# A list scheduler in the source sets the order of every queue of a fused attention and MLP kernel

## The chip, the cores and the metric

The kernel runs on one core of a Trainium2 chip. The metric is the device time of one execution in microseconds. TensorE (PE), VectorE (DVE), ScalarE (ACT), GpSimd (POOL) and SyncE (SP) each work through a queue of their own in order; a wait at the head of a queue holds everything behind it. All DMAs of this kernel are issued by SyncE.

## The reference, cut to what matters

```python
def mab(q, kv):                      # x: 4 x 12480 x 128, inducing: 32 x 128
    s = scale * (q @ kv.T); s = s - s.max(-1)
    a = np.exp(s); a /= a.sum(-1) + 1e-9
    return a @ kv
h = mab(I, x)                        # per batch: 32 x 128
attn = mab(x, h)                     # per batch: 12480 x 128
out = (np.maximum(attn @ w_in, 0) ** 2) @ w_out     # d_ff = 2048
```

The first attention reduces a whole batch to 32 rows h, so nothing of a batch's second half can start before its h is complete. The second attention gives every token 32 weights that sum to one.

## The kernel before, in words

A batch has 26 chunks of 480 tokens (CH), in 7 groups of four (the last of two). The kernel never forms the 2048 hidden columns: since each token is a mix of the 32 rows of h, the squared sum is a form in products of pairs of the 32 weights. There are five kinds of work.

1. **First attention** of batch b (`first`): scores of seven groups (matmuls on x transposed, `xp`), a maximum, exponentials on ScalarE, 32x32 transposes on VectorE (line 356), and row sums on TensorE against the rows of x (line 368), which arrive in 13 half-tiles through five buffers `xnb`. Its end is `hT` (line 385).
2. **Preparation** of batch b (`prepare`): from h and the weights to `w16` (pair weights, four sets of products, line 540, and of sums, line 548), `lin`, `singles`, `osc` and `bias`; long chains of small VectorE steps between TensorE steps.
3. **Second attention** of each group (`second`): scores against h and their transpose into one of 8 slots (line 405), maximum (408), subtraction on POOL (412), exponential (413), sums (416 to 418), product on POOL (419), transpose (422), split into two halves (428, 431), and a store to DRAM `ad` (432).
4. **Squares** of each group (`squares`): three loads of `ad` back as `dT` (450), a matmul (464), VectorE (470), POOL (474), and four stores into `dT` (476).
5. **Chunks** (`Chunk`): two `up` steps of two matmuls into a pair of PSUM banks each (658; there are two pairs), two `lift` steps on ScalarE that square them (668), `down` with five matmuls (674, 675), an eviction with scale and bias on ScalarE (678) or VectorE (680), and a store (681) from a ring of three.

The order is made in two layers. The source emits the chunks in a loop and sprinkles the steps of kinds 1 to 4 between them: a planner (`spread`, `plan`, `background`) gives each step a date in units of chunks, and `background(k)` emits what has come due. `heavy` says by chunk number whether an eviction goes to ScalarE. The framework's own scheduler then sets each queue's order with its model of time; `issue_after` only keeps background steps behind their anchors on the same engine. Batch 0's first attention, with the narrowing of the weights, lies ahead of all this, and batch 0's preparation and first two groups come right behind its h. All loads of the next batch (`xp`, lines 272; rows, 261 and 265) share SyncE's queue with the chunks' stores.

Of the kernel before, what the change touches and what calls it, by code (L numbers as in the profile page):

```python
# [13 lines left out]
AF = mybir.ActivationFunctionType  # L14
ALU = mybir.AluOpType
AX = mybir.AxisListType

P = 128
# [30 lines left out]
def attend_then_relu2_mlp(ctx: ExitStack, tc: tile.TileContext, xn, xT, indT, w_in, w_out, outT):  # L49
# [218 lines left out]
    def load_xT(b, G, again=False):  # L268
        pool, bufs = (mlp, 2) if again else (flow, NX)
        w = WID[G]  # L270
        xp = pool.tile([P, 4 * CH], F32, tag="xp", name=f"xp_{b}_{G}_{again}", bufs=bufs)[:, 0:4 * w]
        nc.sync.dma_start(xp, xT[:, b, 4 * CH * G:4 * CH * G + 4 * w])
        return xp
# [7 lines left out]
    def first(b):  # L281
# [5 lines left out]

        def load_xn(h):

            return load_half(b, h, xnb[h % XB]) if h < HALVES else None  # L290
# [20 lines left out]
        xns = st.rows if not b else {}  # L311
        for G, w in enumerate(WID):
            if b and G == 3:
                xns = {h: load_xn(h) for h in range(XB)}
            if not b:
                turn(G)
# [36 lines left out]
        for G, nb32 in enumerate(BLK):  # L353
# [9 lines left out]
            for t in range(nb32):  # L363
# [7 lines left out]
                if b and (t % 8 == 7 or t == nb32 - 1):  # L371
                    xns[h + XB] = load_xn(h + XB)
# [15 lines left out]
    def second(b, G, again=False):  # L388
# [4 lines left out]
        xp = st.xp.pop(G)  # L393
# [3 lines left out]
        scores(ps, st.hT, xp, w)  # L397

        if again:
            e = work.tile([P, 15, MI], F32, tag="e2", name=f"e2_{b}_{G}")  # L400
        else:
            k = 480 * ((NG * b + G) % SLOTS)
            e = scored[:, k:k + 480].rearrange("p (t i) -> p t i", i=MI)
        ef = e.rearrange("p t i -> p (t i)")
        nc.vector.transpose(ef[:, 0:wb], ps[:, 0:wb])  # L405
        yield
        mx = work.tile([P, 15], F32, tag="mx2", name=f"mx2_{b}_{G}")
        nc.vector.tensor_reduce(mx[:, 0:t], e[:, 0:t], axis=AX.X, op=ALU.max)  # L408
        held["act"] += 100 + 0.833 * wb
        held["dve"] += 5 * (110 + 1.042 * wb) + 400  # L410
        yield
        nc.gpsimd.tensor_tensor(e[:, 0:t], e[:, 0:t], mx[:, 0:t].unsqueeze(2).broadcast_to([P, t, MI]), op=ALU.subtract)  # L412
        nc.scalar.activation(e[:, 0:t], e[:, 0:t], AF.Exp, scale=scale)  # L413
        yield
        z = work.tile([P, 15], F32, tag="z2", name=f"z2_{b}_{G}")
# [4 lines left out]
        yield  # L420
# [3 lines left out]
        if again:  # L424
            nc.scalar.copy(a16[:, 0, 0:w], a[:, 0:w])
            nc.vector.tensor_tensor(a16[:, 1, 0:w], a[:, 0:w], a16[:, 0, 0:w], op=ALU.subtract)
        else:
            nc.vector.tensor_scalar(
                a16[:, 0, 0:w], a[:, 0:w], lessen, None, op0=ALU.add, op1=ALU.min, accum_out=least_d[:, b, G:G + 1],
            )  # L430
            nc.vector.scalar_tensor_tensor(a16[:, 1, 0:w], a[:, 0:w], lessen, a16[:, 0, 0:w], op0=ALU.add, op1=ALU.subtract)
        nc.sync.dma_start(st.ad[:, :, :, 480 * G:480 * G + w].rearrange("q i h n -> (q i) h n"), a16[:, :, 0:w])
        yield
# [20 lines left out]

    def squares(b, G):

        st = sts[b]
        n = GRP[G]
        rows = slice(0, MI * n)
        dT = st.aT[G] = load_dT(b, G)  # L460
        yield
        ps = ps_o.tile([P, 512], F32, tag="po", name=f"sq_{b}_{G}")
        for j in range(n):
            nc.tensor.matmul(  # L464
                ps[MI * j:MI * j + MI, 0:CH].rearrange("p (q t) -> p q t", q=4), st.singles[0:96],
                dT[0:96, :, j * TP:(j + 1) * TP], start=True, stop=True,
            )
        z = mlp.tile([P, CH], F32, tag="z", name=f"z_{b}_{G}", bufs=2)
        held["dve"] += 110 + 1.042 * CH
        nc.vector.tensor_scalar(z[rows], ps[rows, 0:CH], st.off[rows], cut[rows], op0=ALU.add, op1=ALU.max)  # L470
        yield
        g = mlp.tile([P, 4, TP], F16, tag="zz", name=f"zz_{b}_{G}", bufs=2)
        zv = z.rearrange("p (q t) -> p q t", q=4)
        nc.gpsimd.tensor_tensor(g[rows], zv[rows], zv[rows], op=ALU.mult)  # L474
        for j in range(n):
            nc.sync.dma_start(dT[96:P, :, j * TP:(j + 1) * TP], g[MI * j:MI * j + MI])
        yield

    def prepare(b):

        st = sts[b]
        tt, ts, stt = nc.vector.tensor_tensor, nc.vector.tensor_scalar, nc.vector.scalar_tensor_tensor
        held["dve"] += 16000

        ps = side_psum(f"hw_{b}")
        scores(ps, st.hT, w_in_sb, 512)
        hw = flow.tile([P, NF, MI], F32, tag="hw", name=f"hw_{b}", bufs=1)
        nc.vector.transpose(hw.rearrange("p k i -> p (k i)"), ps)
        hws = flow.tile([P, NF, MI], F32, tag="hws", name=f"hws_{b}", bufs=1)
        ssq = small("ssq")  # L490
        nc.scalar.activation(hws.rearrange("p k i -> p (k i)"), ps, AF.Square, accum_out=ssq)
        yield
        ends = work.tile([P, 2, NF], F32, tag="ends", name=f"ends_{b}")
        hi, lo, sm = ends[:, 0], ends[:, 1], small("sum_c", NF)
        cm2 = small("cm2", 3)
        nc.vector.tensor_reduce(sm, hw, axis=AX.X, op=ALU.add)
        bank = side_psum(f"bank_{b}")
        bp = bank[:, 500:508]
        nc.tensor.matmul(bp[:, 0:1], every, ssq, start=True, stop=True)
        mg, nmg, s, k2 = small("mg"), small("nmg"), small("s"), small("k2")  # L500
        root(k2, bp[:, 0:1], 2.0 ** 62)
        nc.vector.reciprocal(s, k2)
        yield
        hw16 = flow.tile([P, NF, 2, MI], F16, tag="hw16", name=f"hw16_{b}", bufs=1)
        for k in range(2):
            nc.scalar.mul(hw16[:, :, k], hw, s)
        hw16f = hw16.rearrange("p k q i -> p k (q i)")
        nc.vector.tensor_reduce(hi, hw, axis=AX.X, op=ALU.max)
        nc.vector.tensor_reduce(lo, hw, axis=AX.X, op=ALU.min)
        ts(hws, hw, s, None, op0=ALU.mult)  # L510
        yield
        ts(mg, k2, 2.0 ** -20, None, op0=ALU.mult)
        ts(nmg, k2, -2.0 ** -20, None, op0=ALU.mult)
        up, dn, pos, mix, inc = (small(n, NF) for n in ("up_c", "dn_c", "pos", "mix", "inc"))
        mean = (1.0 - RHO) / MI
        ts(dn, lo, 0.0, RHO, op0=ALU.min, op1=ALU.mult)
        stt(dn, sm, mean, dn, op0=ALU.mult, op1=ALU.add)
        stt(dn, dn, nmg, lo, op0=ALU.add, op1=ALU.max)
        ts(pos, dn, 0.0, None, op0=ALU.is_ge)
        sp = small("sp", NF)  # L520
        stt(sp, sm, s, pos, op0=ALU.mult, op1=ALU.mult)
# [12 lines left out]
        def products(c):  # L534
# [6 lines left out]
            if c == NQ - 1:  # L541
                nc.vector.tensor_copy(g[:, :, 112:P], hwS[:, :, 0:16])
# [483 lines left out]
```

## Time and profile before

| | us |
|---|---|
| median of 3 runs (lowest, highest) | 431.45 (429.72, 433.61) |
| profiled execution | 429.16 |
| its span, first to last instruction | 427.4 |
| TensorE, VectorE, ScalarE, POOL busy | 355.8, 314.5, 298.4, 86.8 |

Busy time adds the records of one engine without counting overlap twice. TensorE's matmuls are pipelined, so its busy time covers some time in which nothing more was issued than the next matmul needed. The chain of waits follows back from the last instruction to what released each step. In rows of the trace `PE hp L658 x4` is four matmuls of line 658 that write `hp`; `xp_False` is `xp` of batches 1 to 3.

### The profile page before, as it was taken

How to read it: one execution, taken by the hardware profiler on the slowest of the kernel's cores; microseconds unless marked ns; L12 is line 12 of the kernel's file. 1: busy time of each engine (PE TensorE's matmuls, PEld its weight loads, DVE VectorE, ACT ScalarE, POOL GpSimd, SP SyncE). 2: the span in 40 equal slices, each digit the busy share in tenths (PEclk: the TensorE clock that was granted, in tenths of full speed). 3: DMA queues.
4: the chain of work that ended last, by engine and by line, in shares of the span. 5: the costliest groups of instructions: out<-in, count | busy, mean ns of one | idle time of the engine just before them, and what ended most of it. 6: DMA issues, size and time to landing. Idle time of an engine off the chain costs nothing.

```text
span 427.4 us, 8743 instructions
## 1 busy us (share of the span) xinstructions
PE 355.8 (83%) x3077; PEld 169.3 (40%) x3077; DVE 314.5 (74%) x857; ACT 298.4 (70%) x416; POOL 86.8 (20%) x93
## 2 busy tenths in 40 slices
PE   0994648599949989798799698998998898999993
PEld 0753413253414433244444233354443344544441
DVE  8859899969711499999444899995169999664441
ACT  1564330068948887677756798788798997899983
POOL 1000021522100032522000334320014442211000
PEclk9996985679969999999999999999999999999998
DMA  7972666915689786796799797976863256556542
GB/s 276 416 237 76 224 205 234 269 46 160 187 300 307 253 290 207 245 266 198 216 339 294 263 377 259 232 250 210 292 197 96 83 180 196 178 168 187 156 163 99
DMA packets 63765, 94.34 MB, mean 221 GB/s; under 512 B 22880, under 2 KB 53856, under 8 KB 63712
## 3 DMA queue, kind: packets, MB, share of 16 engines
q1 hardware_dynamic: 63712, 93.69, 68.1%
q8 instruction: 26, 0.43, 0.4%
q14 instruction: 27, 0.22, 0.2%
HBM read 58.52 MB, written 31.95 MB: 212 GB/s over the span
## 4 chain that ended last, share of the span: by engine, by line
PE 42%; DVE 29%; DMA 16%; ACT 5%; issue 3%; SPq 2%; POOL 1%; DVEq 0%; ACTq 0%
PE hp L658 13%; PE po L674 12%; DMA xnb<-xn_dram 6%; DMA outT_dram<-o 4%; PE hacc L368 4%; DVE G L540 4%; PE s L277 4%; ACT g L668 3%; PE po L675 3%; PE wq L548 3%; DMA rows<-xn_dram 3%; DVE scored L405 3%; DVE z L416 2%; DMA dT<-ad 2%; DVE mx L408 2%
## 5 line engine op out<-in xcount | busy, mean ns | idle before, releaser
L668 ACT ACTIVATE g<-hp 128x960 f16<-128x960 f32 x208 | 195.1, 973 | 44.6 <-PE hp L658 37.2
L658 PE MATMUL hp<-dT,pairs 96*128 96x480 f16 x416 | 119.0, 371 | 3.4 <-ACT g L668 3.3
L674 PE MATMUL po<-g,w 128*128 128x480 f16 x416 | 113.8, 367 | 3.4 <-DVE z L470 1.8
L474 POOL TENSOR_TENSOR zz<-z 128x480 f16<-128x480 f32 (+1 forms) x28 | 29.5, 1054 | 161.7 <-DVE z L470 107.6
L674 PEld LDWEIGHTS <-w 128*128 128x128 f16 x416 | 39.1, 98 | 53.8 <-issue 15.3
L678 ACT ACTIVATE o<-po,bias,osc 128x480 f32<-128x480 f32 x66 | 49.6, 757 | 12.5 <-DMA outT_dram<-o 8.1
L658 PEld LDWEIGHTS <-pairs 96*128 96x128 f16 x416 | 35.0, 99 | 58.3 <-issue 34.3
L680 DVE TENSOR_SCALAR o<-po,osc,bias 128x480 f32<-128x480 f32 x38 | 29.5, 775 | 35.0 <-PE po L675 27.8
L412 POOL TENSOR_TENSOR scored<-scored,mx 128x480 f32<-128x480 f32 (+1 forms) x28 | 29.6, 1057 | 115.1 <-DVE k L197 56.3
L368 PE MATMUL hacc<-xnb,en 128*32 128x128 f32 x664 | 27.7, 292 | 13.6 <-DMA xnb<-xn_dram 10.6
L675 PE MATMUL po<-dT,lin 128*128 128x480 f16 x104 | 38.2, 367 | 0.0
L419 POOL TENSOR_TENSOR scored<-scored,z 128x480 f32<-128x480 f32 (+1 forms) x28 | 27.2, 972 | 44.8 <-DVE z L418 30.4
L356 DVE STREAM_TRANSPOSE en<-sT 128x480 f32<-128x480 f32 (+1 forms) x28 | 17.7, 638 | 23.8 <-PE hacc L368 22.0
L540 DVE TENSOR_TENSOR G<-hwp,hw 128x512 f16<-128x512 f16 x64 | 28.3, 501 | 1.1 <-PE wq L548 1.1
L413 ACT ACTIVATE scored<-scored 128x480 f32<-128x480 f32 (+1 forms) x28 | 16.2, 579 | 18.3 <-POOL scored L412 18.3
L368 PEld LDWEIGHTS hacc<-xnb,en 128*32 128x32 f32 x664 | 18.8, 115 | 25.3 <-DMA xnb<-xn_dram 13.1
L470 DVE TENSOR_SCALAR z<-sq,off,cut 128x480 f32<-128x480 f32 (+1 forms) x28 | 21.4, 765 | 8.2 <-PE sq L464 7.9
L304 ACT COPY xp<-xt 128x896 f32<-128x896 f32 (+1 forms) x13 | 12.3, 956 | 17.1 <-PE xt L301 17.1
L345 ACT ACTIVATE sT<-sT,nb 128x480 f32<-128x480 f32 (+1 forms) x28 | 18.3, 667 | 7.1 <-DVE nb L338 7.1
L277 PE MATMUL s<-xp_False,indT_sb 128*32 128x480 f32 (+1 forms) x168 | 20.5, 561 | 3.2 <-DMA xp_False<-xT_dram 2.3
L277 PE MATMUL s<-xp_False,hT 128*32 128x480 f32 (+1 forms) x168 | 19.9, 547 | 3.3 <-DVE sT L321 3.1
L321 DVE TENSOR_SCALAR_CACHE_REDUCE sT<-s 128x480 f32<-128x480 f32 (+1 forms) x28 | 17.0, 608 | 5.8 <-PE s L277 5.7
(206 smaller groups left out, 456.0 us busy)
## 6 DMA issues: line engine op xcount, KB each, us to landing
outT_dram<-o SPq DMA_DIRECT2D x104, 240.0 KB, 2.6
xp_False<-xT_dram SPq DMA_DIRECT2D x18, 960.0 KB, 5.3
xnb<-xn_dram SPq DMA_DIRECT2D x21, 512.0 KB, 7.0
xnb<-xn_dram SPq DMA_DIRECT2D x23, 448.0 KB, 6.1
dT<-ad SPq DMA_DIRECT2D x72, 120.0 KB, 3.6
ad<-a SPq DMA_DIRECT2D x24, 240.0 KB, 3.1
dT<-zz SPq DMA_DIRECT2D x104, 30.0 KB, 2.3
wi<-w_in_dram SPq DMA_DIRECT2D x4, 512.0 KB, 5.8
```

What stands on the lines that cost most here:

```text
L277: nc.tensor.matmul(ps[32 * q:32 * q + 32, 0:w], lhsT, xp[:, w * q:w * q + w], start=True, stop=True,)
L368: st.last = nc.tensor.matmul(hacc[32 * q:32 * q + 32, 0:P], en[:, t], xg[:, t % 8], start=G == 0 and t < 4, stop=G == NG - 1 and t + 4 >= ...
L412: nc.gpsimd.tensor_tensor(e[:, 0:t], e[:, 0:t], mx[:, 0:t].unsqueeze(2).broadcast_to([P, t, MI]), op=ALU.subtract)
L419: nc.gpsimd.tensor_tensor(e[:, 0:t], e[:, 0:t], z[:, 0:t].unsqueeze(2).broadcast_to([P, t, MI]), op=ALU.mult)
L474: nc.gpsimd.tensor_tensor(g[rows], zv[rows], zv[rows], op=ALU.mult)
L540: tt(g[:, :, MI * j:MI * j + n], hwp[:, :, 0:n], hw16f[:, :, s0:s0 + n], op=ALU.mult)
L658: last = nc.tensor.matmul(hp[:, i, 0:CH].rearrange("p (q t) -> p q t", q=4), pairs[0:96, (2 * j + i) * P:(2 * j + i + 1) * P], self.dT[0:9 ...
L668: return nc.scalar.activation(self.g[:, 2 * j:2 * j + 2], self.hp.pop(j)[:, 0:2, 0:CH], AF.Square)
L674: nc.tensor.matmul(po[:, 0:CH], st.w16[:, i], self.g[:, i], start=i == 0, stop=False)
L675: done = [nc.tensor.matmul(po[:, 0:CH].rearrange("p (q t) -> p q t", q=4), st.lin, self.dT, start=False, stop=True)]
L678: done.append(nc.scalar.activation(o, po[:, 0:CH], AF.Identity, bias=st.bias, scale=st.osc))
L680: done.append(nc.vector.tensor_scalar(o, po[:, 0:CH], st.osc, st.bias, op0=ALU.mult, op1=ALU.add))
```

## The change

The planner, `heavy`, `background` and the `issue_after` anchors go. The five kinds of work are rewritten as jobs: generators that yield before each step the engine, an assumed duration, a due time, and what it needs, and then emit the step's instructions. `Order.run` keeps a clock per engine and for the DMA, finds the earliest time at which any job could go on, and of the jobs that could go on on that engine within PATIENCE of it takes the one due first. The whole stretch from batch 0's h on is emitted in that order, and `manual_schedule` makes the program's order the order of the queues. Buffer rings are modelled (`Ring`), a cross-engine handover costs LATE, a transfer lands after LAND or behind what is queued. An eviction takes ScalarE or VectorE, whichever is free first. Preparation steps are cut finer and put in another order within a batch; `mx2` and `z2` have 4 buffers instead of 2. `prepare_w_out` is emitted ahead of the ordered stretch. The arithmetic, tiles and transfers stay.

```diff
-HEAVY = 18
-READ = (0, 2, 1, 1)
-REST = 2.6
-LONG, LAG, WEIGHTS = 5, 3, 10
+NO = 3
+PERIOD = 2.95
+LEAD = 33.0
+SLACK = 6.0
+AHEAD = 17
+QUEUED = 3.0
+PATIENCE = 0.12
+SPARE = 0.3
+LAND = 3.2
+LATE = {"PE": 0.25, "ACT": 0.2, "DVE": 0.15, "POOL": 0.25}
...
+    def when(self, job):
+        engines, took, due, needs, alone = job[1]
+        t = 0.0 if alone else job[2]
+        for n in needs:
+            r = n.ready()
+            if r is None:
+                return None
+            t = max(t, r)
+        if engines == "SP":
+            return max(t, self.free["SP"], self.moved - QUEUED), "SP"
+        if "|" in engines:
+            act, dve = max(t, self.free["ACT"]), max(t, self.free["DVE"])
+            return (act, "ACT") if act + SPARE < dve else (dve, "DVE")
+        return max(t, self.free[engines]), engines
+
+    def run(self):
...
+            first, engine = min(w for w, _ in could)
+            (start, engine), job = min(
+                ((w, j) for w, j in could if w[1] == engine and w[0] <= first + PATIENCE), key=lambda x: (x[1][1][2], x[0][0]),
+            )
+            took = job[1][1]
+            if engine == "SP":
+                self.free["SP"] = start + 0.06
+                self.moved = max(self.moved, start) + took
+                end = max(start + LAND, self.moved + LAND - 0.7)
+            else:
+                self.free[engine] = start + took
+                end = start + took + LATE[engine]
...
+    def nominal(n):
+        return LEAD + PERIOD * n
+
+    def h_due(b):
+        return nominal(NCH * b - AHEAD)
...
+    def x_loads():
...
+                end = yield op("SP", 2.6 * w / CH, h_due(b) - 30 - 2.0 * (NG - G), xp_ring, alone=True)
+                sts[b].xp[G] = load_xT(b, G, flow, NX)
...
+    def row_loads():
...
+                end = yield op("SP", 1.4, h_due(b) - 24 + 1.3 * h, xnb_free[i], alone=True)
+                sts[b].rows[h] = load_half(b, h, xnb[i])
...
+    def row_sums(b, zs):
...
+                end = yield op("PE", 0.075 * (t1 - t0), H - 14 + 2.0 * G, *needs)
...
+    def readings():
...
+                X = nominal(NCH * b + 4 * G) - 14 - SLACK
+                due = X - 9
+                if b < NB - 1:
+                    due = min(due, h_due(b + 1) - 32 - 2.0 * (NG - G))
+                end = yield op("PE", 0.85, due, att, mark("h", b))
...
+    def attention(b, G, e, X, since, gone):
...
+        yield op("DVE", 0.6, X - 7, here)
...
+        end = yield op("SP", 0.7, X)
...
+    def squares():
...
+                X = nominal(NCH * b + 4 * G) - 11 - SLACK
+                end = yield op("SP", 1.1, X, mark("ad", b, G), dT_ring, alone=True)
...
+    def square(b, G, n, X, rows, dT):
...
+        end = yield op("SP", 0.12 * n, X + 7)
+        for j in range(n):
+            nc.sync.dma_start(dT[96:P, :, j * TP:(j + 1) * TP], g[MI * j:MI * j + MI])
...
+    def pair_weights(b, F, cast, hw16, hw16f, hwp, hwS, pos, since):
...
+            end = yield op("DVE", 1.4 if c < NQ - 1 else 1.6, F - 20 + 4.0 * c, G_ring)
...
+    def pair_sums(b, c, F, g, since):
...
+        end = yield op("PE", 0.93, F - 16 + 4.0 * c, *needs)
...
+    def ups():
...
+                end = yield op("PE", 0.41, nominal(n - 1.5 + j / 2), hp_ring, mark("dT", b, c // 4), alone=True)
...
+    def lifts():
...
+                end = yield op("ACT", 0.92, nominal(n - 1 + j / 2), mark("up", n, j), *([] if j else [g_ring]), alone=True)
...
+    def downs():
...
+            needs = [mark("g", n), mark("zz", b, c // 4), mark("wq", b), mark("lin", b), po_ring]
+            end = yield op("PE", 1.02, nominal(n + 0.8), *needs, alone=True)
...
+    def evictions():
...
+            end = yield op("ACT|DVE" if n < len(CHUNKS) - 1 else "ACT", 0.7, nominal(n + 1.1), mark("down", n), o_ring, alone=True)
...
+    def stores():
...
+            end = yield op("SP", 0.65, nominal(n + 1.5), mark("out", n), alone=True)
...
+    prepare_w_out()
+    for job in (ups(), lifts(), downs(), evictions(), stores(), readings(), squares(), x_loads(), row_loads(), first_softmax(), smallest()):
+        order.add(job)
     for b in range(NB):
...
+        order.add(prepare(b))
+    with tc.manual_schedule(engines={E.PE, E.Activation, E.DVE, E.Pool, E.SP}):
+        order.run()
```

In a preparation F is `nominal(NCH * b)` and the steps' dues run from F - 34 to F - 14. The jobs `exponents`, `transposes` and `row_sums` are the tail of the first attention; each runs at its own pace.

## Rows read from the trace of the kernel before

**Rows 1.** The page's first part: busy us, share of the span, instructions.

```profile
PE 355.8 (83%) x3077; PEld 169.3 (40%) x3077; DVE 314.5 (74%) x857; ACT 298.4 (70%) x416; POOL 86.8 (20%) x93
```

**Rows 2.** Windows of 10 us: busy us (instructions) per engine, granted clock, DMA share, GB/s.

```profile
120.00:130.00 10.00, 5.10 (x42) 2.26 (x43) 0.68 (x1) 3.79 (x5) 0.00 (x0) 0.66 0.87 320
...
220.00:230.00 10.00, 9.58 (x99) 4.64 (x99) 3.91 (x9) 6.69 (x8) 0.97 (x1) 1.00 0.94 261
...
380.00:390.00 10.00, 10.00 (x53) 4.51 (x51) 4.76 (x7) 9.58 (x11) 0.99 (x1) 1.00 0.64 182
```

**Rows 3.** Chain of waits, whole span: start us, us, what.

```profile
202.13 2.23 DMA outT_dram<-o
...
228.92 8.02 DMA outT_dram<-o
...
293.56 6.23 DMA xnb<-xn_dram
...
391.10 0.81 PE po L674 x4
...
404.05 2.24 DMA outT_dram<-o
```

**Rows 4.** Chain of waits, from 52 to 126 us.

```profile
52.49 0.20 DVE hT L385
...
63.38 2.73 DVE G L540 x8
66.11 0.59 DVE scored L405
...
73.81 3.63 DMA ad<-a
...
78.32 7.46 DMA dT<-ad
...
86.51 1.71 PE hp L658 x4
...
90.73 0.94 PE s L277 x8
...
94.72 0.90 PE wq L548 x16
...
98.49 0.20 PE po L675
...
115.93 2.48 PE hacc L368 x73
118.40 6.45 DMA xnb<-xn_dram
```

**Rows 5.** Instructions of lines 476, 681, 450: issue ns min/median/max, first and last start.

```profile
L476 SPq DMA_DIRECT2D dT<-zz x104: 585/600/1710, 88.4 to 409.6; - x104
...
L681 SPq DMA_DIRECT2D outT_dram<-o x104: 332/376/1475, 101.1 to 421.7; - x104
...
L450 SPq DMA_DIRECT2D dT<-ad x84: 303/427/1487, 77.5 to 397.8; - x84
```

**Rows 6.** The page's DMA issues: count, KB each, median us to landing.

```profile
outT_dram<-o SPq DMA_DIRECT2D x104, 240.0 KB, 2.6
...
xnb<-xn_dram SPq DMA_DIRECT2D x21, 512.0 KB, 7.0
...
dT<-ad SPq DMA_DIRECT2D x72, 120.0 KB, 3.6
```

**Rows 7.** Timeline of SyncE's queue ahead of 228 us: start us, us, what.

```profile
227.12 1.38 SPq L261 DMA_DIRECT2D xnb<-xn_dram  x3
```

**Rows 8.** Groups by line: busy us, mean ns; idle before, releasers.

```profile
L668 ACT ACTIVATE g<-hp 128x960 f16<-128x960 f32 x208 | 195.1, 973 | 44.6 <-PE hp L658 37.2 <-PE po L674 5.9 <-ACT g L668 0.3
...
L678 ACT ACTIVATE o<-po,bias,osc 128x480 f32<-128x480 f32 x66 | 49.6, 757 | 12.5 <-DMA outT_dram<-o 8.1 <-PE po L675 3.4 <-ACT g L668 0.6
...
L680 DVE TENSOR_SCALAR o<-po,osc,bias 128x480 f32<-128x480 f32 x38 | 29.5, 775 | 35.0 <-PE po L675 27.8 <-DMA outT_dram<-o 5.4 <-ACT sT L345 1.6
```

More of the change, by code (lines that the diff above doesn't have):

```diff
@@ new lines, with __init__, add, step @@
+class Order:
+    def __init__(self):
+        self.free = {"PE": 0.0, "ACT": 0.0, "DVE": 0.0, "POOL": 0.0, "SP": 0.0}
+        self.moved = 0.0
+        self.jobs = []
+    def add(self, gen):
+        job = [gen, None, 0.0]
+        self.step(job, None)
+    def step(self, job, end):
+        try:
+            job[1] = job[0].send(end)
+        except StopIteration:
+            return
+        if end is not None:
+            job[2] = end
+        self.jobs.append(job)
+    def when(self, job):
[13 more added lines that the diff above has]
+    def run(self):
+        while self.jobs:
+            could = []
+            for job in self.jobs:
+                w = self.when(job)
+                if w:
+                    could.append((w, job))
+            assert could, "every job waits"
+            first, engine = min(w for w, _ in could)
[10 more added lines that the diff above has]
+                end = start + took + LATE[engine]
+            self.jobs = [j for j in self.jobs if j is not job]
+            self.chosen = engine
+            self.step(job, end)
@@ L48, in attend_then_relu2_mlp, with op @@
+def op(engines, took, due, *needs, alone=False):
+    return engines, took, due, needs, alone
 @with_exitstack
@@ L309, in turn @@
                     nc.scalar.copy(to[:, :, 224:240], ps[:, 7].rearrange("p (q r) -> p q r", q=4)[:, :, 0:16])
-        xns = st.rows if not b else {}
+        xns = st.rows
         for G, w in enumerate(WID):
[L313 to L316, printed above, removed]
+            turn(G)
             ps = att_psum(f"s1_{b}_{G}")
@@ L453, in load_dT @@
         return dT
[L455 to L477, printed above, removed]
@@ new lines, in readings @@
+    def readings():
+        for b in range(NB):
+            st = sts[b]
+            for G in range(NG):
+                w, t = WID[G], BLK[G]
+                wb = 32 * t
+                X = nominal(NCH * b + 4 * G) - 14 - SLACK
[3 more added lines that the diff above has]
+                end = yield op("PE", 0.85, due, att, mark("h", b))
+                done = att.take()
+                ps = att_psum(f"s2_{b}_{G}")
+                scores(ps, st.hT, st.xp.pop(G), w)
+                mark("read", b, G).t = end
+                end = yield op("DVE", 0.62, due + 1, slots)
+                gone = slots.take()
+                k = 480 * ((NG * b + G) % SLOTS)
+                e = scored[:, k:k + 480].rearrange("p (t i) -> p t i", i=MI)
+                if wb > w:
+                    nc.vector.memset(ps[:, w:wb], 0.0)
+                nc.vector.transpose(e.rearrange("p t i -> p (t i)")[:, 0:wb], ps[:, 0:wb])
+                done.t = end
+                order.add(attention(b, G, e, X, end, gone))
@@ new lines, in squares @@
+    def squares():
+        for b in range(NB):
+            st = sts[b]
+            for G, n in enumerate(GRP):
+                X = nominal(NCH * b + 4 * G) - 11 - SLACK
+                rows = slice(0, MI * n)
+                end = yield op("SP", 1.1, X, mark("ad", b, G), dT_ring, alone=True)
+                dT_ring.held.append(mark("over", b, G))
+                dT = st.aT[G] = load_dT(b, G)
+                mark("dT", b, G).t = end
+                order.add(square(b, G, n, X, rows, dT))
@@ new lines, in pair_sums @@
+    def pair_sums(b, c, F, g, since):
+        st = sts[b]
+        here = Mark()
+        here.t = since
+        needs = [here, mark("tsg", b), side if c == 0 else mark("wq", b, c - 1)]
+        end = yield op("PE", 0.93, F - 16 + 4.0 * c, *needs)
+        if c == 0:
+            side.held.append(mark("wq free", b))
+            st.wq = side_psum(f"wq_{b}")
+        for k in range(NF):
+            nc.tensor.matmul(st.wq[:, c * P:c * P + P], g[:, k], w_hi[:, k], start=k == 0, stop=k == NF - 1)
+        mark("G used", b, c).t = end
+        mark("wq", b, c).t = end
+        end = yield op("ACT", 0.32, F - 14 + 4.0 * c, *([mark("over", b - 2, NG - 1)] if b > 1 else []))
+        nc.scalar.mul(st.w16[:, c], st.wq[:, c * P:c * P + P], st.tsg[:, c:c + 1])
+        if c == NQ - 1:
+            mark("wq", b).t = end
```

763 lines of the change are left out of this document (450 added, 313 removed).

## The prediction

> **What bounds the kernel now.** I began with the page's busy times: TensorE 355.8 us, VectorE 314.5, ScalarE 298.4 of a 427.4 us span [rows 1]. No engine fills the span, so I read stretches of 10 us next. In 380:390 TensorE is busy throughout and issues 53 matmuls, while ScalarE works 9.58 of 10 us: this is the rate the kernel reaches when nothing disturbs it. In 120:130 TensorE has 5.10 us and VectorE 0.68 [rows 2]. The busy time hides part of the loss, because matmul records overlap; I count TensorE's work by its spacing in the chain of waits instead. Four matmuls of 480 columns take 0.81 us [rows 3], so a chunk (four up, five down) takes 9 x 0.2025 = 1.82 us and 104 chunks 190 us. The 21 + 28 score groups at 0.94 us, seven of them half size, are 43 us; 39 half-tiles of row sums, some 16 matmuls each, at the burst's 2.48 us for 73 are 21 us; four preparations, with 4 x 0.90 us of pair sums each [rows 4] and about 5.6 us of smaller matmuls by my estimate, are 37 us; squares and small products, also estimated, about 14. Together 305 us after batch 0's h.
>
> h is ready at 52.7 us [rows 4], so 374.7 us remain in the span and about 70 us of TensorE time holds no work. I place it in three parts. **Lead**: from h to the end of chunk 0's first complete output at 98.7 [rows 4] are 46 us with some 24 us of work, so 22 lost. **Middle**: from 98.7 to the issue of the last store at 421.7 [rows 5] are 323 us with 281 of work, so 42 lost. **End**: 5.7 us for that store. The chain names the middle: row sums wait for loaded rows three times, 6.45 us first and 6.23 last, 16.7 together; evictions wait for earlier stores to land five times, 2.23 first, 8.02 the longest, 2.24 last, 17.9 together [rows 3, 4]. These are queueing costs, and order is what this change rewrites. By contrast the matmuls, activations and transfers are the same in number and shape; the arithmetic after h must still fit 305 us of TensorE.
>
> **The change, part by part.**
>
> *Before h nothing moves* except that the preparation of w_out comes first in the program. Its two long activations already run before the square of hw, and h's own chain is not behind them. Taken at 0; if its products came later, each late microsecond would shift everything.
>
> *Lead.* In the old order VectorE does, ahead of the first attention store at 73.81 [rows 4], work that the first chunk's input does not need: five further reading transposes (5 x 0.59 from the chain [rows 4]), the rest of group 1's attention (about 3.2), and the first two sets of pair products (2.73 [rows 4]): 8.9 us. By due times, group 0's attention falls due 6 to 12 us after h, those transposes at 16.5 and later, products at 13 and 17. They go behind. The gain for that store is bounded by 0 (POOL and ScalarE steps of group 0 become exposed, and VectorE idles for them) and 8.9; I take 6, nearer the upper end since independent preparation steps fill the gaps. Then the dT load took 7.46 us there [rows 4] against a median of 3.6 [rows 6]: it shared the DMA with five x loads. The new order starts row loads at once and holds queued transfers to 3 us by its own count; gain between 0 and 3.9, taken at 2. First up: 86.5 - 8 = 78.5. The first output also needs the pair weights; on VectorE about 11 us of later groups' work (transposes, maxima, first scores of batch 1) leaves the way, so it moves by the same 8. Of these, 3 us are score matmuls merely moved into the middle. Net **5 us**.
>
> *Row loads.* The five buffers were filled long before, used in one burst of 73 matmuls in 2.48 us, and the sixth half-tile was only issued when the burst had freed a buffer; hence 6.45 us of standstill [rows 4]. The new order knows a landing time (about 3.9 us for a half-tile), and puts chunk matmuls between. The measured median is 7.0 [rows 6], so some 3 us per round stay uncovered; two rounds in three batches would give back all 16.7. But 7.0 includes the burst's own queue: a half-tile at 1.4 us behind four others accounts for it. I take 6 of 16.7 as left: **gain 10.7**, bounds 0 and 16.7.
>
> *Stores.* A store that lands in 2.6 us [rows 6] cannot stall a ring of three outputs; the 8.02 us one was issued right behind three row loads [rows 3, 7]. Loads dealt out one at a time remove most bursts, while stores still share the queue: 6 of 17.9 left, **gain 11.9**, bounds 0 and 17.9.
>
> *Evictions* choose ScalarE or VectorE by which is free 0.3 us earlier, instead of a fixed stretch per batch. The total does not change: 66 at 757 ns and 38 at 775 ns [rows 8], 79 us. With 195.1 us of lifts ScalarE stays under TensorE's 305. Taken at 0, hidden under TensorE; without that cover up to the 3.4 us by which ScalarE's evictions waited for output matmuls [rows 8].
>
> *SyncE.* No DMA is added, but every one has a new place. The scheduler books 0.06 us of SyncE for an operation; four issues of the squares take 4 x 600 ns, three dT issues 3 x 427, a store 376 [rows 5]. With 104, 84 and 104 of these that is 137 us, with the hundred other transfers, at 0.4 to 0.6 by my estimate, some 182 us of issue in 375, so SyncE is half busy and a wrong place costs up to 2.4 us behind one set of squares. Taken inside the 6 + 6 us left above; its larger price is the first rival.
>
> The Trainium skill, Perfetto Trace Analysis, section "What 'DMA-bound' means", counts a DMA sequencer full of issues as a bound of its own. No row here shows SyncE full, so by that rule the sum is unchanged unless the stretch with loads closes up.
>
> *Sum.* 5 + 10.7 + 11.9 = 27.6 us. The profiled execution took 429.16 us with 427.4 in the span; the median of the three runs is 431.45, 2.3 higher. 431.45 - 27.6 = **404 us**. Check: 305 us of TensorE would then lie in 347 us instead of 375, a share of 88% where 81% stood; 380:390 shows that it can hold more than that.
>
> **Rivals.**
>
> *1. SyncE is late (chance 0.16).* At 404 us the issues fill 182 of 347 us on average, but in stretches with loads nearer two thirds. If one set of squares in each of the 21 groups with loads around it puts 1 us on TensorE through a late load or store, 21 us of the 22.6 in the middle go, and only the lead remains: 431.45 - 6.6 = 425 us. For it: 0.60 us for each of four against 0.06 for all [rows 5]. Against: work is due 20 us ahead of use, a slack that swallows 2.4. A bound by issue, as that section of the Trainium skill has it, would show in the same way.
>
> *2. Loads crowd out stores (chance 0.10), slower.* x and row loads become eligible as soon as their buffers are free. Seven x buffers and five row buffers are 9.2 MB; 220:230 moved 261 GB/s with the DMA engines 0.94 busy [rows 2]. The scheduler assumes some 370 GB/s, and nothing on the chip tells it that transfers run late. It decides where a store takes over three chunk times less an eviction, 3 x 3.0 - 0.8 = 8.2 us; the store at 228.92 took 8.02 [rows 3]. If every third store of the three batches with loads (26 of 78) exceeds that by 1.5 us, 39 us are added; less the 27.6 won, 443 us. Against: the old order had such bursts too, and only five stores of it show in the chain.
>
> *3. Little is changed (chance 0.04).* The old planner also had dates, and its queues were already laid out in advance; if the new order is nearly the same one, 431 us.
>
> **How the numbers follow.** The forecast, that at least half of the middle's 34.6 us and some lead go, has 0.70. Its own range is 388 (both waits gone, 34.6, and the lead's upper bounds, 8.9 + 3.9 less 3 moved: 44) to 424 (all lead bounds at 0 and a fifth of the waits). The range of 8 in 10 drops rival 2 and the lowest corner and takes in rivals 1 and 3 up to 430. One per cent, 4.3 us, is what a measurement here can tell from no change. Faster than 427.1: the forecast and 0.07 of rival 1, 0.77. Same: 0.07 of rival 1, 0.03 of 3, 0.02 of 2, 0.12. Slower: the rest, 0.11.
>
> **What would show it.** Right: first up matmul near 78 us after the start and the first complete output near 90; no 6 us wait of row sums on loads, stores in the chain under 10 us in all; no stretch between 100 and 360 with TensorE near 5 us; lifts at 7 to 8 per 10 us there instead of 4 to 7. The lead is wrong if VectorE idles between group 0's steps and the first store stays near 73. Rival 1 shows as engines waiting for transfers whose issue was queued behind squares; rival 2 as stores landing after 8 us or more, evictions waiting on them. The prediction fails altogether if ScalarE, with 195.1 us of lifts, becomes the engine that others wait for: two pairs of PSUM banks hold lifts and up matmuls in step, and an in-order queue that places another activation too early stops both.

## The result: 427.35 us instead of 431.65, and the profile after

| | before | after |
|---|---|---|
| median (lowest, highest), four executions each on one chip | 431.65 (429.72, 433.61) | 427.35 (426.38, 427.44) |
| ratio [95% interval] | | 0.9895 [0.9848, 0.9942] |
| profiled execution, its span | 429.16, 427.4 | 426.38, 424.6 |

The forecast was 404 us, a gain of 27.6 us; the gain was 4.3. The result lies in the stated range, which reached up to 430 us to take in two rivals. Ratios, here and below, leave out executions over 1.5% above the fastest of their kernel. The page's first part, after, against [rows 1]:

```profile
PE 357.0 (84%) x3077; PEld 169.2 (40%) x3077; DVE 329.9 (78%) x879; ACT 285.4 (67%) x394; POOL 83.3 (20%) x93
```

The groups of the lifts and evictions, after (busy us, mean ns | idle before, releasers), against [rows 8]:

```profile
L1059 ACT ACTIVATE g<-hp 128x960 f16<-128x960 f32 x208 | 193.7, 969 | 63.7 <-PE hp L1045 62.5
...
L1093 DVE TENSOR_SCALAR o<-po,osc,bias 128x480 f32<-128x480 f32 x60 | 46.1, 768 | 44.8 <-PE po L1075 34.2 <-DMA outT_dram<-o 3.9 <-PE s L369 3.1
L1091 ACT ACTIVATE o<-po,bias,osc 128x480 f32<-128x480 f32 x44 | 33.1, 755 | 11.2 <-PE po L1075 4.1 <-DMA dT<-ad 2.3 <-DVE a L779 2.2
```

Evictions stand 44 to 60 where they stood 66 to 38, and ScalarE waits 62.5 us for up matmuls instead of 37.2. No engine fills the span; TensorE's share, 84%, is the highest. The chain of waits, after (start us, us, what): the lead, then all its waits for a DMA behind the lead, against [rows 3, 4].

```profile
53.53 1.06 PE hw L369 x8
...
77.81 0.89 PE hp L1045 x2
...
88.96 0.20 PE po L1075
...
103.23 2.67 DMA ad<-a
...
108.05 2.50 DMA dT<-ad
...
117.78 5.16 DMA xnb<-xn_dram
...
173.63 6.23 DMA ad<-a
...
180.78 4.21 DMA dT<-ad
...
202.55 3.89 DMA outT_dram<-o
...
210.60 5.75 DMA xnb<-xn_dram
216.41 6.61 DMA xnb<-xn_dram
...
268.42 6.20 DMA ad<-a
...
275.53 3.51 DMA dT<-ad
...
297.47 5.88 DMA xnb<-xn_dram
...
378.45 2.67 DMA dT<-ad
...
386.54 2.45 DMA outT_dram<-o
...
398.29 2.88 DMA dT<-ad
```

The first up stands at 77.81 (before 86.51), the first output at 88.96 (98.49): the lead came. So did its mechanism: the first store of attention was issued at 65.2 us where it stood at 73.81.

```profile
L781 SPq DMA_DIRECT2D ad<-a x28: 567/576/1398, 65.2 to 396.0; - x28
```

Stores are in the chain with 3.89 + 2.45 = 6.3 us (17.9). But the rows have 23.4 us (16.7), and attention that is stored (`ad`) and loaded again (`dT`) has 30.9 us; the chain of before had one such pair, 3.63 + 7.46 = 11.1 us, in its lead, and none behind it.

Waits in a chain do not add up to a difference of times (run e17 below takes about the time of after, and its chain has 34.3 us of waits for rows and 26.0 for stores), so I use a second reading: the start of the first lift of a chunk (the records of the lift's line, two to a chunk). Tail means from chunk 72 to chunk 103.

| | chunk 0 | chunk 72 | chunk 103 | tail |
|---|---|---|---|---|
| before | 87.5 | 351.0 | 418.2 | 67.2 |
| after | 78.7 | 334.7 | 416.0 | 81.3 |
| after is ahead by | 8.8 | 16.3 | 2.2 | -14.1 |

The lead gave 8.8, the middle 7.5, and the tail took 14.1 back. Windows of the lift's line alone show the tail, before and then after (us, ScalarE busy, lifts, granted clock, DMA share, GB/s):

```profile
380.00:400.00 20.00, 19.10 (x21) 1.00 0.67 196
400.00:420.00 20.00, 18.12 (x20) 1.00 0.40 135
```

```profile
380.00:400.00 20.00, 14.08 (x17) 1.00 0.61 185
400.00:420.00 20.00, 15.56 (x18) 1.00 0.47 157
```

One thing that sets it apart is the date of batch 3's h. The transpose of `hw` follows h at once; its four executions, before and after (min/median/max ns, first and last start):

```profile
L488 DVE STREAM_TRANSPOSE hw<-hw x4: 717/717/718, 53.9 to 314.5; 128x512 f32<-128x512 f32 x4
```

```profile
L838 DVE STREAM_TRANSPOSE hw<-hw x4: 705/716/718, 54.7 to 324.1; 128x512 f32<-128x512 f32 x4
```

Batch 3 begins with chunk 78. Before, its h stood there when 61 chunks had begun, after when 69 had; so preparation, seven groups of attention and their squares fall into the last 100 us, beside the last chunks. The scheduler's own clock has it there too (69, tail 77.3): it takes whatever can start, and chunks can.

### The profile page after: what moved, and what is told of

It reads as the page before. It is cut to its first block, busy times and chain, and to the rows that moved or that the text cites. A ratio compares the mean times of both kernels' runs of the same rounds, so it can differ in the third digit from the quotient of the medians.

```text
span 424.6 us, 8741 instructions
## 1 busy us (share of the span) xinstructions
PE 357.0 (84%) x3077; PEld 169.2 (40%) x3077; DVE 329.9 (78%) x879; ACT 285.4 (67%) x394; POOL 83.3 (20%) x93
## 2 busy tenths in 40 slices
DMA packets 63760, 94.29 MB, mean 222 GB/s; under 512 B 22880, under 2 KB 53856, under 8 KB 63712
## 3 DMA queue, kind: packets, MB, share of 16 engines
q1 hardware_dynamic: 63712, 93.69, 66.9%
## 4 chain that ended last, share of the span: by engine, by line
PE 46%; DVE 25%; DMA 16%; ACT 6%; issue 4%; SPq 2%; DVEq 0%; ACTq 0%
PE po L1074 12%; PE hp L1045 11%; DMA xnb<-xn_dram 7%; PE s L369 7%; DMA dT<-ad 4%; DMA ad<-a 4%; PE hacc L694 4%; DVE G L1008 3%; ACT g L1059 3%; PE po L1075 3%; PE xt L391 2%; DVE scored L741 2%; DMA outT_dram<-o 1%; DVE o L1093 1%; PE sq L805 1%
## 5 line engine op out<-in xcount | busy, mean ns | idle before, releaser
L1059 ACT ACTIVATE g<-hp 128x960 f16<-128x960 f32 x208 | 193.7, 969 | 63.7 <-PE hp L1045 62.5
L1045 PE MATMUL hp<-dT,pairs 96*128 96x480 f16 x416 | 111.3, 371 | 6.2 <-ACT g L1059 6.0
L1074 PE MATMUL po<-g,w 128*128 128x480 f16 x416 | 104.0, 372 | 0.9 <-DVE o L1093 0.8
L1093 DVE TENSOR_SCALAR o<-po,osc,bias 128x480 f32<-128x480 f32 x60 | 46.1, 768 | 44.8 <-PE po L1075 34.2
L1091 ACT ACTIVATE o<-po,bias,osc 128x480 f32<-128x480 f32 x44 | 33.1, 755 | 11.2 <-PE po L1075 4.1
L369 PE MATMUL s<-xp,hT 128*32 128x480 f32 (+1 forms) x224 | 28.3, 579 | 2.4 <-DVE scored L741 2.3
L369 PE MATMUL s<-xp,indT_sb 128*32 128x480 f32 (+1 forms) x224 | 27.1, 555 | 1.6 <-DVE sT L408 0.9
L694 PEld LDWEIGHTS hacc<-xnb,en 128*32 128x32 f32 x588 | 15.8, 111 | 21.9 <-DVE en L671 7.4
L1008 DVE TENSOR_TENSOR G<-hwp,hw 128x512 f16<-128x512 f16 x64 | 23.8, 431 | 0.6 <-PE wq L1024 0.5
L779 DVE SCALAR_TENSOR_TENSOR a<-a,lessen,a 128x480 f16<-128x480 f32 (+1 forms) x28 | 20.5, 733 | 1.0
L671 DVE STREAM_TRANSPOSE en<-sT 128x480 f32<-128x480 f32 (+1 forms) x21 | 13.0, 632 | 9.2 <-PE hacc L694 9.0
L1024 PE MATMUL wq<-w_hi,G 128*128 128x128 f16 x256 | 16.9, 219 | 2.1 <-ACT w L1028 1.0
```

What stands on the lines that cost most here:

```text
L369: nc.tensor.matmul(ps[32 * q:32 * q + 32, 0:w], lhsT, xp[:, w * q:w * q + w], start=True, stop=True,)
L694: nc.tensor.matmul(hacc[32 * q:32 * q + 32, 0:P], st.en[G][:, t], xg[:, t % 8], start=G == 0 and t < 4, stop=G == NG - 1 and t + 4 >= nb32,)
L1008: nc.vector.tensor_tensor(g[:, :, MI * j:MI * j + n], hwp[:, :, 0:n], hw16f[:, :, s0:s0 + n], op=ALU.mult)
L1045: nc.tensor.matmul(hp[:, i, 0:CH].rearrange("p (q t) -> p q t", q=4), pairs[0:96, (2 * j + i) * P:(2 * j + i + 1) * P], dT[0:96], start=Tr ...
L1059: nc.scalar.activation(gs[n][:, 2 * j:2 * j + 2], hps.pop((n, j))[:, 0:2, 0:CH], AF.Square)
L1074: nc.tensor.matmul(po[:, 0:CH], st.w16[:, i], g[:, i], start=i == 0, stop=False)
```

## The experiments

All medians in us; ratios [95%] are to the kernel before, run beside it on the same chip (its medians there were 427 to 428.5, so ratios are what to compare; after stands at 0.9895). Chunk columns are from one profiled execution, which can lie some us off the median (e3: 420.63). Runs e8 and e15 stand in the text alone.

| run | median | ratio | chunk 0 | chunk 72 | tail |
|---|---|---|---|---|---|
| e1 five row loads, after | 416.92 | 0.9719 [0.9662, 0.9775] | 78.0 | 326.1 | 82.8 |
| e2 five row loads, before | 405.45 | 0.9482 [0.9427, 0.9537] | 87.1 | 329.9 | 63.7 |
| e3 landings as seen | 424.45 | 0.9898 [0.9849, 0.9947] | 84.8 | 326.7 | 83.0 |
| e4 batch 3 early by 30 | 440.01 | 1.0256 [1.0190, 1.0322] | 76.6 | 341.9 | 89.0 |
| e5 evictions to ScalarE | 434.04 | 1.0206 [1.0132, 1.0280] | 78.0 | 337.1 | 85.9 |
| e6 AHEAD 28 | 416.08 | 0.9746 [0.9662, 0.9831] | 89.5 | 335.5 | 72.1 |
| e7 e3 + AHEAD 28 | 415.42 | 0.9749 [0.9679, 0.9819] | 99.5 | 329.5 | 76.2 |
| e9 h of 2 and 3 earlier | 427.16 | 0.9976 [0.9930, 1.0023] | 78.2 | 340.2 | 78.9 |
| e10 landings, h earlier | 416.07 | 0.9724 [0.9652, 0.9796] | 77.1 | 331.2 | 74.8 |
| e11 e1 + h earlier | 413.24 | 0.9671 [0.9605, 0.9737] | 76.6 | 322.8 | 78.7 |
| e12 h of 3 later | 436.69 | 1.0241 [1.0144, 1.0339] | 76.0 | 332.4 | 94.4 |
| e13 landings, dates | 409.10 | 0.9540 [0.9456, 0.9623] | 78.1 | 327.2 | 73.8 |
| e14 squares by GpSimd | 415.43 | 0.9707 [0.9622, 0.9791] | 76.4 | 324.7 | 78.7 |
| e16 e13 + e14 | 399.64 | 0.9344 [0.9277, 0.9411] | 77.6 | 316.8 | 71.4 |
| e17 issue time booked | 424.78 | 0.9899 [0.9825, 0.9973] | 78.1 | 337.6 | 79.3 |
| e18 e16 without dates | 411.61 | 0.9598 [0.9528, 0.9667] | 79.3 | 322.2 | 79.7 |

### What the row loads cost either order: e1, e2

```diff
+                if h >= XB:            # after; before: the same in load_xn
+                    sts[b].rows[h] = xnb[(0, 3, 2, 1, 4, 3)[h % 6]]
+                    continue
```

> The kernel after, but of the 13 half-tiles of rows of batches 1 to 3 only the first five are loaded; the other eight row sums read tiles that already lie in SBUF, so h of these batches is computed from wrong rows (the part left out is 24 of 39 row loads, 12.6 MB). Theory A (transfers that land later than the scheduler books are what ate the gain of the middle): the waits of row sums, 23.4 us in the chain of waits, go, and attention loads that share the queue with them land sooner: 427 - 23 = 404 us, at least below 415. Theory B (VectorE, which now takes 60 instead of 38 evictions, is what others wait for): 425 to 428. Theory D (batch 3's attention is left too late and stretches the last 60 us): a gain in the middle is kept up to the tail, so 404 to 415 too, but with lifts still at 8 to 10 per 10 us at the end.

> The kernel before with the same 24 row loads left out (h of batches 1 to 3 from wrong rows). It tells what the old order lost to these loads. By my sum on record, 16.7 us of row waits and the stores held up behind row loads, 8 to 10 us: 431.5 - 25 = 407 us. If the old order loses as much to them as the new one, the ratio of the two kernels without these loads is the same 0.99 as with them, and the new order's handling of loads is worth nothing. If theory A is right only for the new order, this kernel gains less (415 to 420) than the new one does.

These kernels leave out 24 of 39 row loads. The old order gains 5.2%, 22 us; the new one 0.9719 / 0.9895, 1.8%, 7.6 us. So the price that the prediction put on loads was there, and leaving them out helps the new order a third as much; whether it pays less for them or something else holds it then is not separated. Theory A in its first form falls all the same: without those loads the old order is the better one by 11.5 us, and its tail alone is 19.1 us shorter. Lifts in windows of about the same distance from the end, e2 and then e1:

```profile
340.00:360.00 20.00, 18.46 (x21) 1.00 0.60 181
360.00:380.00 20.00, 18.38 (x21) 1.00 0.59 171
```

```profile
360.00:380.00 20.00, 13.66 (x16) 1.00 0.58 169
380.00:400.00 20.00, 14.80 (x17) 0.91 0.57 175
```

### The scheduler's figures: e3, e17

```diff
-                self.free["SP"] = start + 0.06
+                self.free["SP"] = start + issue      # 0.4 to 2.6 by kind; e17 only this
-                self.moved = max(self.moved, start) + took
-                end = max(start + LAND, self.moved + LAND - 0.7)
+                self.moved = max(self.moved, start) + slower * took
+                end = max(start + land, self.moved + LAND - 0.7)
```

> The kernel after with only the scheduler's figures for SyncE and the DMA changed to what the trace of after shows: issue times of 0.4 to 2.6 us instead of 0.06, x and row loads 1.3 times as long, landings of 6.0 (x), 5.9 (rows), 4.2 (loads and stores of the squares) us. The instructions are the same, in another order. The scheduler's own clock ends at 349.9 instead of 337.3 us after h. Theory A: the chip now follows its clock, the slip of 30 us shrinks to 10 or less, so 53.5 + 349.9 + 10 + 3 = 416 us, and row waits in the chain fall under 10 us. Theory C (the loads themselves take that time whatever the order): 424 to 430, the waits only move. Theory B: 425 to 430.

> The kernel after with one figure of the scheduler put right: an operation of SyncE is booked with 0.4 to 2.6 us of its queue (2.6 for the four issues of a set of squares) instead of 0.06; lengths and landings of transfers stay as they were. The scheduler's clock hardly changes (337.4 instead of 337.3). If the wrong figure was the price, the order now avoids the queueing and the gain is that of e14: 413 to 417 us. If the issue time itself is the price, or the landings under load, there is no gain: 421 to 427.

In after the lifts fall 30 us behind the scheduler's clock by the end; in e3 by 11, about what theory A said (10 or less), and the waits for rows in its chain fall to 13.1 us (it said under 10). Yet the time is that of after, not theory A's 416: the clock itself is 12.6 us longer. What had been an unforeseen wait became a foreseen one. Booking the issue time alone (e17) changes nothing either. With the dates of after, wrong figures explain where the chip stands still, not how long it takes; with other dates they can count (e9 against e10, below) or not (e6 against e7).

### Evictions: e5, e8

```diff
-            return (act, "ACT") if act + SPARE < dve else (dve, "DVE")
+            return (dve, "DVE") if dve + SPARE < act else (act, "ACT")
```

> The kernel after with the preference of evictions turned round: ScalarE unless VectorE is free 0.3 us earlier. By the scheduler 70 evictions on ScalarE instead of 44, so VectorE is relieved of 26 x 0.77 = 20 us; its own clock ends 2.2 us later (339.5). Theory B (VectorE, 330 us busy, is what the new order waits for): 427 - 10 to 20 = 407 to 417 us, most of it in the middle. Theory D (h of batch 3 comes too late: in after it comes at chunk 69 and the last 31 chunks take 81 us, in the kernel before they take 67) and theory A (landings): no change, 424 to 431 us, with the last 31 chunks still at 78 us or more.

70 evictions went to ScalarE and the kernel became 3% slower than after. Theory B expected 10 to 20 us less from relieving VectorE, and falls, at least where ScalarE takes the evictions. 

> AHEAD 26, SLACK 9 (attention and squares due 3 us earlier) and evictions to ScalarE first (66), in one kernel. The scheduler's clock ends at 330.5. Theory D: like e6, 418 to 421. B and D together: under 412. A alone: 425 to 431.

 It gave 421.70 us, 0.9805 [0.9741, 0.9868]: by the ratios 4% better than e5 with its earlier dates, and less of a gain than e6 below has without the evictions.

### The date of the last h: e4, e6, e7, e9, e11, e12

```diff
-AHEAD = 17
+AHEAD = 28                                       # e6, e7
-        return nominal(NCH * b - AHEAD)
+        return nominal(NCH * b - (0, 17, 27, 27)[b])   # e9, e11; e12: (0, 17, 17, 8)
-                X = nominal(NCH * b + 4 * G) - 14 - SLACK
+                X = nominal(NCH * b + 4 * G) - 14 - SLACK - (EARLY if b == NB - 1 else 0.0)   # e4: 30; squares too
```

> The opposite of e9 for batch 3 alone: its h due only 8 chunks ahead (after: 17). Scheduler's clock: h of batch 3 at 258.9 (chunk 76) instead of 244.4, the last 31 chunks 91.4 instead of 77.3, the end 346.5 instead of 337.3. Theory D: the tail grows to 93 to 96 us and the time to 427 + 9 to 12 = 436 to 440. If other things set the tail, 424 to 430.

> The kernel after with AHEAD 28 instead of 17: h of batches 1 to 3 is due 28 chunks ahead of the batch's first chunk. The scheduler's own clock: h of batch 3 at 227.5 instead of 244.4 us after h of batch 0 (at chunk 62 instead of 69), the first lift 9 us later (31.8 instead of 23.0), chunk 72 at the same time, the last 31 chunks in 70.2 instead of 77.3, the end at 328.0 instead of 337.3. Theory D: the chip follows, the last 31 chunks take 72 to 75 instead of 81 us and the time is 427 - 7 to 9 = 418 to 420. Theory A or B alone: whatever the tail gains is lost in the middle to loads or VectorE, 424 to 431.

> The landings and issue times as the trace shows them (e3) and AHEAD 28 together. The scheduler's clock ends at 343.2 (e3: 349.9), the last 31 chunks take 75.6 (79.6). If A and D both hold and add up: e3 less 7 us, about 414 to 418 us, with the chip behind the scheduler's clock by no more than the 11 us of e3. If the tail is not set by the date of h: like e3, 423 to 425.

Both directions came as theory D said, in the tail and in the time: 94.4 us with the h later (`hw` at 341.9), 72.1 with it earlier, although e6 throws the lead away (chunk 0 at 89.5; last `hw` at 304.3). The last start of `hw` in e12:

```profile
L838 DVE STREAM_TRANSPOSE hw<-hw x4: 705/712/717, 53.3 to 341.9; 128x512 f32<-128x512 f32 x4
```

> The kernel after with the second attention and the squares of batch 3 due 30 us earlier; nothing else changes. Theory D: the two waits of squares on loads in the tail (378.45 and 398.29, 5.5 us) go and the last 28 chunks run at 10 to 11 lifts per 10 us instead of 8 to 10, so 427 - 6 = 421 us. Theory A: the work only moves forward into the stretch with loads and stretches that; the scheduler's own clock is 7.5 us longer, so 427 to 435 us.

> The kernel after with h of batches 2 and 3 due 27 chunks ahead instead of 17, batch 1 left at 17, so that the lead is that of after. Scheduler's clock: first lift as in after (23.1), h of batch 3 at 225.3 us (chunk 60) instead of 244.4 (chunk 69), the last 31 chunks 71.5 instead of 77.3, the end 333.0 instead of 337.3. Theory D (the late h of batch 3 sets the tail): first lift near 78.5 as in after, the last 31 chunks in 72 to 75 instead of 81 us, time 418 to 421, or 408 if the lead that e6 gave up (11 us) comes on top of e6. Against D: 424 or more, or a tail still at 80 us.

> e1 (24 of 39 row loads left out, h of batches 1 to 3 from wrong rows) with h of batches 2 and 3 due 27 chunks ahead. e1 lost to the old order without these loads (417 against 405 us) in the last 31 chunks: 82.8 against 63.8 us. Theory D: the tail falls to 72 to 75 us and the time to 406 to 410; so row loads and the late h together are what the new order lost. Against D: the tail stays, or the time moves back into the middle: 414 to 418.

These three missed. e4 asks for the work of batch 3 earlier while its h stays late (`hw` at 326.7); chunk 72 comes 7.2 us later than in after and the tail grows by 7.7. That the work crowds the same stretch is my reading, not shown. In e9 `hw` starts at 308.2 instead of 324.1 and the tail is still 78.9, with chunk 72 later too; waits of `dT` on `ad` in its chain are 34.0 us instead of 15.8. So an early h is not enough by itself. e11 shows one thing that can hold the tail then: its chain at 382 us.

```profile
382.09 0.96 POOL zz L824
383.06 0.02 issue
383.07 0.60 SPq L827
...
385.16 0.60 SPq L827
...
386.44 0.43 SPq L516
...
386.91 2.41 DMA dT<-ad
```

A load of attention (line 516) stands in SyncE's queue behind four issues of the squares (827), which wait for GpSimd. Those issues are 2.55 us of its whole chain, so much of its tail (78.7) stays unexplained.

### SyncE's queue: e14, e15

```diff
-            nc.sync.dma_start(dT[96:P, :, j * TP:(j + 1) * TP], g[MI * j:MI * j + MI])
+            nc.gpsimd.dma_start(dT[96:P, :, j * TP:(j + 1) * TP], g[MI * j:MI * j + MI])
```

> The kernel after with the 104 transfers of the squares into dT issued by GpSimd instead of SyncE, at the same places of the order. Takes 104 x 0.6 = 62 us of issue out of SyncE's queue, and GpSimd, 83 us busy, has room. Rival 1 (SyncE late: attention loads and stores wait behind these issues): the new waits of dT on ad go, 427 - 10 to 20 = 407 to 417 us. Theory that the dates are too tight or the transfers themselves land late: 424 to 428, and slower (430 to 435) if a transfer issued by GpSimd lands later than one issued by SyncE.

> The same in the kernel before, whose order was laid out by another planner. If SyncE's issue is a price that only the new order pays, this one does not gain: 429 to 433. If both pay it, both gain the same. If transfers issued by GpSimd land later, this one loses about as much as e14 does.

e14 gains 0.9707 / 0.9895, 1.9%, 8 us; in the profiled execution 10 us of lead at chunk 72 (324.7 instead of 334.7) and 2.6 in the tail. Row waits in its chain are 13.5 us instead of 23.4, though the rows themselves land no sooner (medians 7.2 and 6.6 us instead of 6.8 and 5.9); the waits on `ad` and `dT`, which the expectation had going, are 27.0 instead of 30.9. Adding the records of SyncE's queue behind 53 us, after issues for 197 us of 371, 65 of them for these transfers, and e14 for 124. Besides, in after these issues held SyncE's queue while they waited for GpSimd's squares (total us, times, longest):

```profile
SPq L822 <- POOL zz L819: 19.4, 10, 4.1
```

e14 takes both the issues and these waits out of the queue, and no run separates the two. e15 had a median of 427.16 (418.57 to 430.06) against 428.52: its spread is several times the difference, and whether the old order pays the same stays open. The transfers and the DMA queues, after and then e14:

```profile
q1 hardware_dynamic: 63712, 93.69, 66.9%
...
dT<-zz SPq DMA_DIRECT2D x104, 30.0 KB, 2.0
```

```profile
q1 hardware_dynamic: 48736, 90.49, 65.6%
q0 software_dynamic: 3328, 3.20, 3.6%
...
dT<-zz POOLq DMA_DIRECT2D x104, 30.0 KB, 2.9
```

They land later (2.9 instead of 2.0 us), and the DMA engines' time is the same (66.9% of 424.6 is 284 us, 69.2% of 412.7 is 286), so it is the queue that was relieved. Not every wait of the chain is of that kind. In SyncE's timeline of after, the store of `ad` at 173.63 is issued as soon as VectorE has its data (173.62), so the squares ahead of it cost it nothing; it stands between two x loads and lands 6.23 us later, and the `dT` loads follow at 179.93.

```profile
172.94 0.54 SPq L364 DMA_DIRECT2D xp<-xT_dram  x1
173.63 0.57 SPq L781 DMA_DIRECT2D ad<-a  x1
174.42 0.43 SPq L364 DMA_DIRECT2D xp<-xT_dram  x1
...
179.93 1.28 SPq L516 DMA_DIRECT2D dT<-ad  x3
```

### All together: e10, e13, e16, e18

e10 is e9 with the figures of e3 (x loads as booked before, landing 5.0). e13 has the dates (0, 17, 22, 26) and EARLY 6; e16 adds e14 to it; e18 is e16 without the dates.

> e9 with the scheduler's figures for SyncE and transfers as the trace shows them, but x loads left at the old length with 5.0 us landing, so that the lead is not given up (first lift 24.9 by the scheduler's clock). It ends at 343.9. If A and D add up and the slip stays at the 11 to 17 us of e3 and e7: 53.5 + 343.9 + 13 + 2 = 412 us, or 405 if the lead of after (8 us) is kept and the middle of e7 is reached. If the lead is always lost again later: 415 as e7.

> The figures of e10, h of batches 2 and 3 due 22 and 26 chunks ahead (batch 1: 17), and batch 3's attention and squares due 6 us earlier. Scheduler's clock: first lift 24.9, h of batch 3 at 230.4 (chunk 61), the last 31 chunks 73.1, the end 335.9 (e10: 343.9, e3: 349.9). If order alone decides and the slip is again 11 to 17 us: 53.5 + 335.9 + 14 + 2 = 405 to 408 us. If what is won by dates is lost to transfers that crowd each other: 414 to 418 as e7 and e10.

> e13 and e14 together, with the scheduler's issue time for these transfers set back to 0.06. Scheduler's clock: 335.4. If SyncE's issue is a price: below e13 by 5 us or more, near 400. If not: e13 within 3 us, or slower by what the other queue costs in e14.

> e16 (transfers booked as seen, squares issued by GpSimd) with the due dates of after: h 17 chunks ahead for every batch, nothing due earlier in batch 3. Scheduler's clock: 343.5 instead of 335.4, h of batch 3 at 249.5 (chunk 69), the last 31 chunks 78.1 instead of 72.3. Theory D: e16 + 8, 406 to 409 us, with the loss in the last 31 chunks. If the dates are worth nothing once SyncE is relieved: 398 to 401.

e16 beats both kernels: 6.6% under before, 5.6% under after (0.9344 / 0.9895). Of the 431.65 us of the result, 0.9344 is 403 us: with dates, figures and queue put right, the new order gives about what the forecast had. It keeps the lead (77.6), has a tail of 71.4 and h of batch 3 by 281.4. Its page (POOL's time includes 57.9 us of issuing), then the only wait for a DMA left in its chain from h to the end of the ups:

```profile
PE 348.9 (88%) x3077; PEld 166.5 (42%) x3077; DVE 334.8 (84%) x886; ACT 279.5 (71%) x387; POOL 138.8 (35%) x197
```

```profile
136.27 7.97 DMA outT_dram<-o
```

The figures alone (e3, 0.9898) and e9's dates alone (0.9976) gain nothing over after, and the two together (e10, 0.9724) gain 1.7%. Against e18 the dates are worth 2.6% (11 us, 8.3 of them in the tail), against e13 the queue 2.1%; the figures add to e14 a per cent that the intervals (e14, e18) do not separate. No run went further. In e6, e9, e11, e13 and e16 h of batch 3 stands there when 59 to 61 chunks have begun, about as in the old order (61), and their tails still run from 71.4 to 78.9 us; what holds them above its 64 to 67 us stays open.

## Why the prediction was right and wrong

The sum was 5 for the lead and 10.7 + 11.9 for the middle, with no term for the last chunks. By the starts of the chunks the lead gave 8.8, the middle 7.5 up to chunk 72, and the tail took 14.1 back. So the lead held, the middle was mis-sized, and a term that stood at nothing without a reason was the only stretch that lost time. The prediction's own sign of the middle did not come either: between 100 and 360 us, lifts stand at 3 to 9 per 10 us, 148 in all where before had 143.

**Lead.** Predicted 5 us net with the first up at 78.5 and the first output near 90; measured 77.81 and 88.96. Right, and so was the mechanism: the store of attention came 8.6 us earlier (6 taken, 8.9 the bound), and chunk 0 is 8.8 us ahead where the sum had 8 less 3 paid back later.

**Stores.** Predicted 17.9 to 6 in the chain; measured 6.3, and the longest landing of a store fell from 10.1 to 7.4 us. Right for this chain, in part by luck: e17, as fast as after, has 26.0 there. That 11.9 us of time came of it is not shown.

**Row loads.** "I take 6 of 16.7 as left" is the step that failed in the chain: 23.4 are there. Its reading of the cost was right (e2: 22 us for the old order); leaving the loads out gives the new order 7.6 (e1). What failed is the inference that a scheduler that knows a landing time covers it: it booked 3.9 us where the loads take 5.9 to 6.8, and when it was told (e3) its waits fell to 13.1 us but the time did not, since the order itself became longer. Only with e9's dates as well (e10) did the right figures pay.

**SyncE.** "Taken inside the 6 + 6 us left above" was wrong; rival 1, which put the price of the queue's place at 21 us and the time at 425, gave the result within 3 us, with a chance of only 0.16. That its time came out is partly luck, since it put nothing on the tail. Its mechanism is shown in part: 8 us, not 21, come back when the 104 issues leave the queue. "Work is due 20 us ahead of use, a slack that swallows 2.4" was the reason against it, and wrong: from `ad` to an up matmul lie a store, three issues, a load, VectorE, GpSimd, four issues and another landing. The Trainium skill, Perfetto Trace Analysis, section "What 'DMA-bound' means", asks for an issuing track solid with DMA work. Here SyncE's was 53% full (197 of 371 us) and still cost 8 us: here the queue cost by what stood behind an issue, not by being full. By the Trainium skill, Trainium Kernel Development and Optimization, section "Key Constraints", issuing from several engines saves only the sequencer's issue time. e14 agrees in that the DMA engines' time is unchanged. What it saved was not issue time alone: 19.4 us of waits for GpSimd left SyncE's queue with the 65 us of issues, and the 8 us are the worth of both.

**The tail.** This is the other step that failed: no term of the sum and no rival spoke of it, and it lost 14.1 us. The end was counted at 5.7 us for the last store. But `h_due` with AHEAD 17 stood in the diff, and in the old trace h of batch 3 was there 17 chunks ahead as well, so even on time the new order was no earlier; the chip and the scheduler's own clock delivered it 9 ahead. A check of the sum against TensorE's 305 us could not see this: the work is the same, but what is left for the end is a chain. That the date moves the tail is shown by e12 (later: 94.4), e6 (earlier: 72.1) and e16 against e18 (71.4 and 79.7); that it is not the whole of it, by e9 (`hw` at 308.2, tail 78.9).

**The rest.** Rival 2 did not come (no store of a chunk took 8 us to land), nor did rival 3, nor did ScalarE become the bound. On evictions, taken at 0, e5 tells only that more of them on ScalarE cost 7 us by the medians and 13 by the ratios.

## What to carry to other kernels

A list scheduler that starts whatever can start favoured the plentiful work here and started the last stage's chain late: read where each stage's first result falls, in units of the work around it, and give the last one its own date. A gain by chunk 72 is no gain at the end; mark the same piece of work in both traces at several places before summing waits. Before changing an order, look what stands behind each slow issue in an in-order queue, and try that issue on another queue if one is idle. Try repairs together too: two that gain nothing alone can gain together.

## What the chip showed unexpectedly

The same 104 transfers of 30 KB, issued by GpSimd instead of SyncE, took 0.55 us of issue each (0.60), landed in 2.9 us instead of 2.0, and moved in 3,328 packets of a queue of their own; the whole run had 52,064 instead of 63,712 packets in the data queues. Two stores of 240 KB, issued 0.7 and 1.6 us behind a 960 KB load and with another following, landed in 6.2 us instead of the median of 2.6 (after, at 173.63 and 268.42).
